# Three reorderings in a one-core Trainium2 kernel for layer norm, linear attention and an MLP

## The chip, the cores and the metric

The kernel runs as one program on one core of one Trainium2 chip. A core has four compute engines that each take their instructions in order: TensorE (PE) multiplies matrices, with its weight loads shown apart as PEld, VectorE (DVE) and ScalarE (ACT) work element by element and read PE's result banks (PSUM), and GpSimd (POOL) works element by element on the other on-chip memory (SBUF). SyncE (SP) issues the DMAs. [...] The metric is the device time of one execution in microseconds (us); a smaller number is better.

## The reference

`x` holds 2048 tokens of 640 features. Everything is float32.

```python
x = A_x
xn = _layernorm(x, axis=-1)
return x + _A_ref(xn, A_wqkv, A_w_phi, A_wo) + _B_ref(xn, B_w1, B_b1, B_w2, B_b2)

def _A_ref(x, wqkv, w_phi, wo):                    # 32 heads of 20
    qkv = (x @ wqkv).reshape(B, S, 3, H, Dh)...    # q, k, v
    pq = jnp.einsum("bhsd,hdf->bhsf", q, w_phi)
    pk = jnp.einsum("bhsd,hdf->bhsf", k, w_phi)
    phi_q = jnp.concatenate([_softmax(pq), _softmax(-pq)], axis=-1)
    phi_k = jnp.concatenate([_softmax(pk), _softmax(-pk)], axis=-1)
    kv = jnp.einsum("bhsf,bhsd->bhfd", phi_k, v)
    z  = jnp.einsum("bhsf->bhf", phi_k)
    num = jnp.einsum("bhqf,bhfd->bhqd", phi_q, kv)
    den = jnp.einsum("bhqf,bhf->bhq", phi_q, z)[..., None] + 1e-6
    return (num / den).reshape(B, S, D) @ wo

def _B_ref(x, w1, b1, w2, b2):                     # 640 -> 1728 -> 640
    y = _layernorm(x, axis=-1)
    h = _gelu(jnp.einsum("bsd,df->bsf", y, w1) + b1)
    return jnp.einsum("bsf,fd->bsd", h, w2) + b2
```

## The kernel before

Every float32 operand of a product is split into a high part (an ACT copy to the multiplication format) and a low part (source minus high part, on DVE or POOL; line 58, L1025, L959). A product is then three matmuls, high by high, high by low and low by high, and stands in the profile as lines 64, 65 and 66 (`mm3`). Tokens are worked on in four blocks of 512 (`b` = 0 to 3), or in 16 tiles of 128 (`t` = 0 to 15).

There are four stages in time.

1. The MLP for blocks 0 and 1, up to about 243 us, with the preparation of the attention weights beside it.
2. The projections to keys, values and queries, tile by tile, up to about 437 us. The list `(t, i)` in the code sets the order of PE: `i` = 0 is the main part of k, 1 the rest of k, the rest of q and part of v, 2 the rest of v, 3 the main part of q. For k, `k_tile` builds the two softmaxes: minimum and maximum on DVE (L630, L631), subtractions on POOL (L641), one exponential on ACT (L642), row sums and reciprocal on DVE (L644, L650), one product on POOL (L652), then the split into `ft` or `w1`. For q, `q_tile` does the same with its own subtractions (L641) and products (L691, L693), and transposes on DVE (L699). `kv_tile(t)` multiplies the finished features of k by v and sums them over tokens in five PSUM banks (L672) and one extra bank (L676); it runs some tiles later than the tile's projection. The sum of the last tile, `kv_tile(15)`, runs behind the first two hidden chunks of block 2.
3. The MLP for blocks 2 and 3 from about 437 to 662 us (`passes(g, b, ws)`, `g` = 0 to 6, two hidden chunks of 128 each), with the attention (`attend`, `Attention`) beside it. A hidden chunk takes 15 matmuls into one of the three banks of `ptile`, the same three that the projections use in turn, and `gelu` (L252) empties the bank.
4. The output projection from 662 us to the end (`plain`, `half_size`). Each `mm3` advances a step counter (`advance`); work of other engines is issued at given steps. Blocks 2 and 3 use sums and differences of tokens and of weights (`sums`, `weight_sums`), which save some of the products. `plain` uses two banks in turn; `gather` (L1163) adds a bank to the result on DVE, and that bank's next product waits for it.

In stages 1, 3 (from `g` = 1) and 4 the four compute engines keep the order of the code. In stage 2 and at its end only PE does; DVE, ACT and POOL are ordered there by a scheduler (SP throughout), which `tc.issue_after(x)` ties to an instruction `x`. In `finish_kv` and around it, the subtractions of the last q tile (`subs["q", 15]`) are such ties: the second part of a weight split (`late.pop()()`) and a memset of `kvs` (L809) come behind them. The first MLP pass of stage 3 is tied behind `exps["q", 15]`, the last exponential, since `gelu` needs another table on ACT.

Of the kernel before, what the change touches and what calls it, by code (L numbers as in the profile page):

```python
# [11 lines left out]
ALU = mybir.AluOpType  # L12
# [3 lines left out]
P = 128  # L16
S, D, F, H, DH = 2048, 640, 1728, 32, 20
KC = D // P
# [27 lines left out]
def tile_kernel(ctx: ExitStack, tc: tile.TileContext, x, xT, wkT, wqT, wv, wphi, wo, w1, b1, w2, b2,  # L46
                ident, mmask, emask, vsel, out):
    nc = tc.nc
# [267 lines left out]
    wc, parts, dmas = {}, {}, {}  # L316
# [266 lines left out]
    a = ExitStack()  # L583
# [8 lines left out]
    vbuf = []  # L592
# [17 lines left out]
    turn, exps, subs = [0], {}, {}  # L610
# [14 lines left out]
    def features(t, n):  # L625

        turn[0] += 1
        p3 = pks[0 if n == "k" else 1 + t % 3].rearrange("p (h f) -> p h f", f=DH)
        mx = kp.tile([P, 2, H], F32, name="mx")
        nc.vector.tensor_reduce(mx[:, 0, :], p3, axis=AX, op=ALU.max)  # L630
        nc.vector.tensor_reduce(mx[:, 1, :], p3, axis=AX, op=ALU.min)  # L631
        e = mtile(turn[0] % 3)
        e4 = e.rearrange("p s (h f) -> p s h f", f=DH)
        parts = [(slice(0, H), e4)] if n == "k" else by_head(e.rearrange("p s f -> p (s f)"), DH)
        for hs, ep in parts:
            for s, (a, b) in enumerate(((p3, mx[:, 0, :].unsqueeze(2).to_broadcast([P, H, DH])),
                                        (mx[:, 1, :].unsqueeze(2).to_broadcast([P, H, DH]), p3))):
# [3 lines left out]
                subs[n, t] = nc.gpsimd.tensor_tensor(ep[:, s], a, b, op=ALU.subtract)  # L641
        exps[n, t] = nc.scalar.activation(e, e, AF.Exp, scale=rs_all[:, t:t + 1])  # L642
        sm = kp.tile([P, 2 * H], F32, name="sm")
        nc.vector.tensor_reduce(sm, e.rearrange("p s (h f) -> p (s h) f", f=DH), axis=AX, op=ALU.add)  # L644
        return e, sm

    def k_tile(t):
        e, sm = features(t, "k")
        w = kp.tile([P, 2 * H], F32, name="w")
        nc.vector.reciprocal(w, sm)  # L650
        e3 = e.rearrange("p s (h f) -> p (s h) f", f=DH)
        nc.gpsimd.tensor_tensor(e3, e3, w.unsqueeze(2).to_broadcast([P, 2 * H, DH]), op=ALU.mult)  # L652
# [54 lines left out]
    fts, ets = {}, {}  # L707
# [3 lines left out]
    for t, i in [(t, i) for t in range(13) for i in range(4)] + [(13, 0), (13, 1), (13, 2), (14, 0), (14, 1), (13, 3), (14, 2), (15, 0), (15, 1),  # L711
                                                                  (14, 3), (15, 3), (15, 2)]:
        if (t, i) in ((4, 0), (8, 0)):
            b = t // 4 + 1
            y[b] = [yp.tile([P, KC, 512], F32R, name=f"y{p}{b % 2}") for p in range(2)]
            for p in range(2):
                nc.sync.dma_start(f(y[b][p]), y_dram[b - 2][p])
        ps = proj(t, i)
        pq = 1 + t % 3
        if i == 0:  # L720
            evac = evacuate(ps, 0, slice(1, 17))
        elif i == 1:
            evac = evacuate(ps[:, :F2], 0, slice(17, 20))
            evacuate(ps[:, F2:2 * F2], pq, slice(17, 20))
            v_parts(t, (ps[:, 2 * F2:], 0, 5, G3))
            fts[t] = k_tile(t)
        elif i == 2:
            v_parts(t, (ps[:, :15 * DH], 5, 5, G3), (ps[:, 15 * DH:17 * DH], 10, 1, 2 * DH))
        else:
            evac = evacuate(ps, pq, slice(1, 17))  # L730
            q_tile(t)

        tk = 14 if (t, i) == (15, 2) else t - 2 if t > 1 and i == 0 else None
        if tk is not None:
            kv_tile(tk, fts.pop(tk), vbuf[tk % 2])
        if t and t % 4 == 0:
            store_phi(t // 4 - 1, i)
        if i == 0 and t in (1, 2, 3, 6, 7):

            kc = (1, 2, 3, 6, 7).index(t)  # L740
            lo = rp.tile([P, D], F32, name="r1")
            hi = rp.tile([P, D], F32R, name="r2")
            nc.sync.dma_start(lo, wo[kc * P:(kc + 1) * P, :])
            with tc.issue_after(evac):
                split(hi, lo.bitcast(F32R), lo, eng=nc.gpsimd)
            for w, wd in zip((f(hi), lo), wo_dram):
                nc.sync.dma_start(wd[:, kc, :], w)
        if (t, i) == (11, 0):
            mlp = Mlp((0, 2, 3, 1), ((1, 2), (0, 3)))
            mlp.ph = ptile  # L750
            mlp.fetch(0)
        if (t, i) == (12, 3):
            with tc.issue_after(evac):
                ws = [mlp.take(0)]
            mlp.fetch(1)
        if (t, i) == (15, 3):
            w, late = mlp.take_parts(1)
            ws.append(w)
            late.pop(0)()
# [255 lines left out]
    def tokens(ap):  # L1015
        return ap.rearrange("p (q t n) -> p t q n", q=4, t=4)
# [4 lines left out]
    def hi(t, src, eng=None):  # L1021
        return lambda: nc.scalar.activation(t[0], src, AF.Copy)

    def lo(t, src, eng):
        return lambda: eng.tensor_tensor(t[1], src, f(t[0]), op=ALU.subtract)  # L1025

    def add(eng, out, a, op, b):
        return lambda: eng.tensor_tensor(out, a, b, op=op)
# [9 lines left out]
    def weight_sums(j, start):  # L1038

        w, g = weights[j], nc.gpsimd  # L1040
        if j == 0:
            for n in ("s1", "s2", "s3", "s4", "d5"):
                w[n] = own(ep.tile([P, 512], F32R, name="e", bufs=6), 1 if n == "d5" else 2)
        s = [late[1][:, i * 256:i * 256 + 256].rearrange("p (k n) -> p k n", k=2) for i in range(2)]
        a11, a12, a15, a21, a22, a25 = (late[0][:, j, c, m:m + P] for m in (0, P) for c in (k1, k2, slice(4, 5)))
        events = []
        for n, when, out, x, op, z in (("s1", 0, s[0], a21, ALU.add, a22), ("s2", 1, s[1], s[0], ALU.subtract, a11),
                                       ("s3", 6, s[0], a11, ALU.subtract, a21), ("s4", 9, s[0], a12, ALU.subtract, s[1]),
                                       ("d5", 10, s[1][:, 0:1], a15, ALU.subtract, a25)):
            when += start  # L1050
            events += [(when, add(g, out, x, op, z)), (when + 2, hi(w[n], out)), (when + 2.5, lo(w[n], out, g))]
        return at_steps(*events)

    at = {}
# [42 lines left out]
    def sums():  # L1097
# [18 lines left out]

        v = nc.vector

        def parts(at_, t, src, eng, lag):
            for k in range(2):  # L1120
                part = [by_tile(x[:, k, :]) for x in t]
                yield at_ + k, hi(part, tokens(src[:, k, :]))
                yield at_ + k + lag, lo(part, tokens(src[:, k, :]), eng)

        t1, t2, t3, t4 = tsum
        events = [(0, add(v, q[0], o3[:, k1], ALU.subtract, o2[:, k1])), (3, add(v, q[1], o3[:, k2], ALU.subtract, q[0])),
                  *parts(4, t1, q[0], v, 2), *parts(11, t2, q[1], v, 2),
                  (15, add(v, q[0], o3[:, k2], ALU.subtract, o3[:, k1])), *parts(18, t3, q[0], v, 2),
                  (17, add(v, q[1], o2[:, k2], ALU.subtract, q[1])), *parts(22, t4, q[1], v, 2)]
        return both(at_steps(*events), weight_sums(1, 8))  # L1130

    def late_split(b):
# [13 lines left out]
    def advance():  # L1146
        nonlocal step
        step += 1
        next(mlp.beside, None)
        for n, at_ in enumerate((3, 28), 1):  # L1150
            if step - at_ in range(KC + 1):
                at[n].split(step - at_, nc.vector)
        if step == 18:
            finish(mlp.beside)
            running.append(sums())
        if step == 51:
            running.append(late_split(3))
        for r in running:
            next(r, None)
# [117 lines left out]
```

## Time and profile before

| what | before |
|---|---|
| time, median of 3 runs | 734.23 us (734.23 to 734.6) |
| the profiled execution's own time | 734.7 us |
| its span, first to last instruction | 732.9 us |
| instructions | 9792 |
| DVE busy | 495.2 us (68%) |
| ACT busy | 330.3 us (45%) |
| POOL busy | 386.4 us (53%) |
| mean DMA rate | 132 GB/s |

The span is what the instructions cover; 1.8 us of the execution lie around it. Times in rows of a timeline are counted from the span's start. In such a row stand the start, the duration, the engine, the line and operation, what is written from what, shapes and a count, and in brackets how long the engine stood idle before it and what ended that. Consecutive instructions of one kind are merged into a row with a count, and how many depends on the stretch that was asked for.

### The profile page before, as it was taken

How to read it: one execution, taken by the hardware profiler on the slowest of the kernel's cores; microseconds unless marked ns; L12 is line 12 of the kernel's file. 1: busy time of each engine (PE TensorE's matmuls, PEld its weight loads, DVE VectorE, ACT ScalarE, POOL GpSimd, SP SyncE). 2: the span in 40 equal slices, each digit the busy share in tenths (PEclk: the TensorE clock that was granted, in tenths of full speed). 3: DMA queues.
4: the chain of work that ended last, by engine and by line, in shares of the span. 5: the costliest groups of instructions: out<-in, count | busy, mean ns of one | idle time of the engine just before them, and what ended most of it. 6: DMA issues, size and time to landing. Idle time of an engine off the chain costs nothing.

```text
span 732.9 us, 9792 instructions
## 1 busy us (share of the span) xinstructions
PE 718.2 (98%) x3428; PEld 602.0 (82%) x3428; DVE 495.2 (68%) x823; ACT 330.3 (45%) x567; POOL 386.4 (53%) x342
## 2 busy tenths in 40 slices
PE   8999999999999999999999996999999999999998
PEld 7788887788888888888888885888878888878787
DVE  7848445787653897897887886435565656777853
ACT  7623543434314553553544556156555556550410
POOL 2211312556103887887879789145576777543300
PEclk9999999999999999999999998999999999999999
DMA  9905466545152234534403407933433443153122
GB/s 324 268 20 158 123 194 188 175 166 205 49 216 90 90 111 131 156 134 129 97 1 68 112 18 236 251 111 112 126 108 119 119 140 108 46 226 117 72 86 87
DMA packets 67145, 96.86 MB, mean 132 GB/s; under 512 B 14656, under 2 KB 37840, under 8 KB 65472
## 3 DMA queue, kind: packets, MB, share of 16 engines
q1 hardware_dynamic: 66808, 96.23, 42.2%
q8 instruction: 27, 0.44, 0.3%
q14 instruction: 22, 0.18, 0.1%
q10 hardware_dynamic: 288, 0.01, 0.0%
HBM read 65.87 MB, written 30.35 MB: 131 GB/s over the span
## 4 chain that ended last, share of the span: by engine, by line
PE 89%; DVE 5%; ACT 3%; DMA 1%; issue 1%; POOL 1%; SPq 0%; ACTq 0%; POOLq 0%
PE bank L64 26%; PE bank L65 26%; PE bank L66 26%; PE bank L672 3%; PE bank L459 2%; PE bank L894 1%; PE bank L893 1%; DMA xb<-in_x 1%; DVE m L58 1%; DVE st L130 1%; DMA r<-in_w 1%; DVE y L959 1%; PE bank L829 1%; ACT m L252 1%; DVE y L58 0%
## 5 line engine op out<-in xcount | busy, mean ns | idle before, releaser
L58 POOL TENSOR_TENSOR w<-r,w 128x640 fp32r<-128x640 f32 x52 | 83.4, 1620 | 119.7 <-ACT w L55 90.4
L64 PE MATMUL bank<-y,w 128*128 128x512 f32 (+1 forms) x310 | 122.3, 395 | 1.2 <-DVE ob L1163 1.2
L66 PE MATMUL bank<-y,w 128*128 128x512 f32 (+1 forms) x310 | 121.1, 390 | 0.0
L65 PE MATMUL bank<-y,w 128*128 128x512 f32 (+1 forms) x310 | 120.9, 390 | 0.0
L64 PE MATMUL bank<-m,w 128*128 128x512 f32 x266 | 106.2, 399 | 2.0 <-DVE acc L297 1.3
L66 PE MATMUL bank<-m,w 128*128 128x512 f32 x266 | 104.2, 392 | 0.0
L65 PE MATMUL bank<-m,w 128*128 128x512 f32 x262 | 102.4, 391 | 0.0
L297 DVE TENSOR_TENSOR acc<-bank,acc 128x512 f32<-128x512 f32 x120 | 80.8, 682 | 17.1 <-PE bank L66 12.2
L64 PE MATMUL bank<-wkh,y 128*128 128x512 f32 (+2 forms) x240 | 87.7, 365 | 0.0
L65 PE MATMUL bank<-wkl,y 128*128 128x512 f32 (+2 forms) x240 | 87.2, 363 | 0.0
L66 PE MATMUL bank<-wkh,y 128*128 128x512 f32 (+2 forms) x240 | 86.8, 362 | 0.0
L58 DVE TENSOR_TENSOR m<-m,m 128x512 fp32r<-128x512 f32 (+1 forms) x54 | 45.3, 839 | 55.9 <-ACT m L55 55.9
L64 PEld LDWEIGHTS bank<-y,w 128*128 128x128 f32 x310 | 58.9, 190 | 13.5 <-DVE ob L1163 1.6
L66 PEld LDWEIGHTS bank<-y,w 128*128 128x128 f32 x310 | 58.6, 189 | 12.3
L65 PEld LDWEIGHTS bank<-y,w 128*128 128x128 f32 x310 | 58.8, 190 | 12.0
L641 POOL TENSOR_TENSOR m<-m,mx 128x640 f32<-128x640 f32 (+2 forms) x48 | 43.3, 917 | 42.7 <-DVE mx L630 42.7
L623 ACT ACTIVATE m<-bank 128x512 f32<-128x512 f32 (+1 forms) x64 | 26.4, 439 | 86.4 <-PE bank L66 60.6
L887 POOL TENSOR_TENSOR e<-e,m 120x512 fp32r<-120x512 f32 (+1 forms) x28 | 38.0, 1359 | 48.5 <-ACT m L886 45.7
L64 PEld LDWEIGHTS bank<-m,w 128*128 128x128 f32 x266 | 50.0, 188 | 14.4 <-DVE acc L297 3.3
L252 ACT ACTIVATE m<-bank,b1t 128x512 f32<-128x512 f32 (+1 forms) x54 | 36.2, 672 | 51.6 <-PE bank L66 49.0
L644 DVE TENSOR_REDUCE sm<-m 128x64 f32<-128x1280 f32 x32 | 47.3, 1479 | 17.9 <-ACT m L642 17.7
L66 PEld LDWEIGHTS bank<-m,w 128*128 128x128 f32 x266 | 49.9, 188 | 10.7
(211 smaller groups left out, 1483.4 us busy)
## 6 DMA issues: line engine op xcount, KB each, us to landing
r<-in_w SPq DMA_DIRECT2D x52, 320.0 KB
e<-e SPq DMA_DIRECT2D x40, 240.0 KB
e<-acc SPq DMA_DIRECT2D x52, 160.0 KB
acc<-in_xT SPq DMA_DIRECT2D x4, 1280.0 KB
xb<-in_x SPq DMA_DIRECT2D x8, 320.0 KB
t<-in_x SPq DMA_DIRECT2D x8, 320.0 KB
raw<-in_xT SPq DMA_DIRECT2D x10, 256.0 KB
yh<-t SPq DMA_DIRECT2D x10, 256.0 KB
```

Of the source, the lines that this page charges most:

```text
L58: eng.tensor_tensor(lo, src, f(hi), op=ALU.subtract)
L64: nc.tensor.matmul(ps, lh, rh, start=first, stop=False, **kw)
L65: nc.tensor.matmul(ps, lh, rl, start=False, stop=False, **kw)
L66: nc.tensor.matmul(ps, ll, rh, start=False, stop=last, **kw)
L252: nc.scalar.activation(gt, pz, AF.Gelu_apprx_tanh, bias=b1t[:, 2 * g + j:2 * g + j + 1])
L297: nc.vector.tensor_tensor(acc[b][:, m, :], pw, acc[b][:, m, :], op=ALU.add)
L459: nc.tensor.matmul(ps[:, i * kd:(i + 1) * kd], raw[:kk, (k + i) * P:(k + i + 1) * P], wpt[:kk, g, :nh, 1:], start=True, stop=True)
L623: return nc.scalar.activation(p3[:, :, c], ps.rearrange("p (h f) -> p h f", h=H), AF.Copy).ins
L641: subs[n, t] = nc.gpsimd.tensor_tensor(ep[:, s], a, b, op=ALU.subtract)
L644: nc.vector.tensor_reduce(sm, e.rearrange("p s (h f) -> p (s h) f", f=DH), axis=AX, op=ALU.add)
L672: nc.tensor.matmul(kvp[g // 2][:VM, (g % 2) * 240:(g % 2) * 240 + 240].rearrange("p (s f) -> p s f", s=4), v[:, g * VS:g * VS + VM], ft[:, ...
L887: nc.gpsimd.tensor_tensor(pl, e, f(ph), op=ALU.subtract)
```

## The change

First, the four subtractions of the last q tile are issued behind the POOL product of the last k tile (`muls[15]`). Second, `kv_tile(12)` moves from behind projection (14, 0) to behind projection (14, 1), and so takes the next bank of `ptile` for its extra sums. Third, in stage 4 the token sums and their splits are issued at other steps: from step 10 instead of 18, each sum with its two splits as a group, five steps apart; the splits of block 2 (`at[2].split`) move from steps 28 to 33 to six single steps from 31 to 41; the splits of the weight sums come 3 and 4 steps behind their sum instead of 2 and 2.5, with some sums later.

```diff
@@ features
-                subs[n, t] = nc.gpsimd.tensor_tensor(ep[:, s], a, b, op=ALU.subtract)
+                with tc.issue_after(muls[15]) if (n, t) == ("q", 15) else ExitStack():
+                    subs[n, t] = nc.gpsimd.tensor_tensor(ep[:, s], a, b, op=ALU.subtract)
@@ k_tile
-        nc.gpsimd.tensor_tensor(e3, e3, w.unsqueeze(2).to_broadcast([P, 2 * H, DH]), op=ALU.mult)
+        muls[t] = nc.gpsimd.tensor_tensor(e3, e3, w.unsqueeze(2).to_broadcast([P, 2 * H, DH]), op=ALU.mult).ins
@@ projections
         ps = proj(t, i)
+        if (t, i) == (14, 1):
+            kv_tile(12, fts.pop(12), vbuf[0])
...
-        tk = 14 if (t, i) == (15, 2) else t - 2 if t > 1 and i == 0 else None
+        tk = {(15, 2): 14, (14, 0): None}.get((t, i), t - 2 if t > 1 and i == 0 else None)
@@ weight_sums
-                                       ("s3", 6, s[0], a11, ALU.subtract, a21), ("s4", 9, s[0], a12, ALU.subtract, s[1]),
-                                       ("d5", 10, s[1][:, 0:1], a15, ALU.subtract, a25)):
+                                       ("s3", 7, s[0], a11, ALU.subtract, a21), ("s4", 12, s[0], a12, ALU.subtract, s[1]),
+                                       ("d5", 13, s[1][:, 0:1], a15, ALU.subtract, a25)):
...
-            events += [(when, add(g, out, x, op, z)), (when + 2, hi(w[n], out)), (when + 2.5, lo(w[n], out, g))]
+            events += [(when, add(g, out, x, op, z)), (when + 3, hi(w[n], out)), (when + 4, lo(w[n], out, g))]
@@ sums
-                yield at_ + k, hi(part, tokens(src[:, k, :]))
-                yield at_ + k + lag, lo(part, tokens(src[:, k, :]), eng)
+                yield at_, hi(part, tokens(src[:, k, :]))
+                yield at_ + 2 + k, lo(part, tokens(src[:, k, :]), v)
...
-        events = [(0, add(v, q[0], o3[:, k1], ALU.subtract, o2[:, k1])), (3, add(v, q[1], o3[:, k2], ALU.subtract, q[0])),
-                  *parts(4, t1, q[0], v, 2), *parts(11, t2, q[1], v, 2),
-                  (15, add(v, q[0], o3[:, k2], ALU.subtract, o3[:, k1])), *parts(18, t3, q[0], v, 2),
-                  (17, add(v, q[1], o2[:, k2], ALU.subtract, q[1])), *parts(22, t4, q[1], v, 2)]
+        events = [(1, add(v, q[0], o3[:, k1], ALU.subtract, o2[:, k1])), *parts(1, t1, q[0]),
+                  (6, add(v, q[1], o3[:, k2], ALU.subtract, q[0])), *parts(6, t2, q[1]),
+                  (11, add(v, q[0], o3[:, k2], ALU.subtract, o3[:, k1])), *parts(11, t3, q[0]),
+                  (16, add(v, q[1], o2[:, k2], ALU.subtract, q[1])), *parts(16, t4, q[1])]
@@ advance
-        for n, at_ in enumerate((3, 28), 1):
-            if step - at_ in range(KC + 1):
-                at[n].split(step - at_, nc.vector)
-        if step == 18:
+        for b, steps in ((1, (3, 4, 5, 6, 7, 8)), (2, (31, 32, 33, 36, 37, 41))):
+            if step in steps:
+                at[b].split(steps.index(step), nc.vector)
+        if step == 10:
```

POOL at the end of stage 2, before. `m_3994` are the features of k of tile 15, `m_4026` and `m_4064` those of q of tiles 14 and 15, `w_4082` is a weight chunk of the MLP.

```order
L58 TENSOR_TENSOR w_4082<-r_3729,w_4082 128x640
L641 TENSOR_TENSOR m_4064<-m_2047,mx 128x10x60
L641 TENSOR_TENSOR m_4064<-m_2047,mx 128x40
L641 TENSOR_TENSOR m_4064<-mx,m_2047 128x10x60
L641 TENSOR_TENSOR m_4064<-mx,m_2047 128x40
L58 TENSOR_TENSOR w_4082<-r_3730,w_4082 128x640
L809 MEMSET kvs 120x1408
L652 TENSOR_TENSOR m_3994<-m_3994,w 128x1280
```

The same place in the changed kernel, where the line numbers are larger by 1 to 3:

```order
L58 TENSOR_TENSOR w_4082<-r_3729,w_4082 128x640
L653 TENSOR_TENSOR m_3994<-m_3994,w 128x1280
L642 TENSOR_TENSOR m_4064<-m_2047,mx 128x10x60
L642 TENSOR_TENSOR m_4064<-mx,m_2047 128x10x60
L642 TENSOR_TENSOR m_4064<-m_2047,mx 128x40
L642 TENSOR_TENSOR m_4064<-mx,m_2047 128x40
L58 TENSOR_TENSOR w_4082<-r_3730,w_4082 128x640
L812 MEMSET kvs 120x1408
```

The product of k has moved from behind six instructions to ahead of them. On ACT at that place, before, `m_4143` are the first hidden chunks of block 2 behind `gelu`, `ft` is the high part of the features of k of tile 15, and `r_4120`, `r_4121` are loaded weights:

```order
L55 ACTIVATE w_4209<-r_4120 128x640
L642 ACTIVATE m_4064<-m_4064,rs_all 128x1280
L252 ACT_TABLE_LOAD
L252 ACTIVATE m_4143<-bank_4145,b1t 128x512
L252 ACTIVATE m_4143<-bank_4165,b1t 128x512
L55 ACTIVATE m_4164<-m_4143 128x512
L55 ACTIVATE ft<-m_3994 128x1280
```

And in the changed kernel:

```order
L643 ACTIVATE m_4026<-m_4026,rs_all 128x1280
L55 ACTIVATE ft<-m_3994 128x1280
L643 ACTIVATE m_4064<-m_4064,rs_all 128x1280
L252 ACT_TABLE_LOAD
L252 ACTIVATE m_4143<-bank_4145,b1t 128x512
L252 ACTIVATE m_4143<-bank_4165,b1t 128x512
L803 ACTIVATE t_4199<-bank_2022 127x480
```

The copy of `ft` now stands ahead of the last exponential and of the table load, and the copy of the loaded weights `r_4120` stands further back, where the two rows of `w_4209` follow the hidden chunks. On SP the two 1280 KB loads of `acc` (L300) now stand ahead of the load of `r_4120` (L214) instead of behind it; the stores of the q features (L705) follow as before, save that the load of `r_4215` (L215), ahead of all of them before, now stands behind the third.

DVE in stage 4, before; L1163 are the additions to the result, L1028 the sums of tokens, L1025 the splits of the sums, L959 the splits of block 2:

```order
L1163 TENSOR_TENSOR ob_6059<-bank_6139,ob_6059 128x512
L959 TENSOR_TENSOR y_6152<-acc_5095,y_6151 128x512
L1025 TENSOR_TENSOR m_6104<-w_6097,m_6100 128x512
L959 TENSOR_TENSOR y_6152<-acc_5095,y_6151 128x512
L1025 TENSOR_TENSOR m_6104<-w_6097,m_6100 128x512
L959 TENSOR_TENSOR y_6152<-acc_5095,y_6151 128x512
L1028 TENSOR_TENSOR w_6097<-acc_5433 128x1024
L1028 TENSOR_TENSOR w_6097<-acc_5095,w_6097 128x1024
L1163 TENSOR_TENSOR ob_6059<-bank_6172,ob_6059 128x512
```

In the changed kernel, from the second to the sixth addition (here L1166; L1031 are the sums, L1028 the splits):

```order
L1166 TENSOR_TENSOR ob_5948<-bank_6044,ob_5948 128x512
L1031 TENSOR_TENSOR w_6067<-acc_5433,acc_5095 128x1024
L1028 TENSOR_TENSOR m_6073<-w_6067,m_6069 128x512 x2
L1166 TENSOR_TENSOR ob_5948<-bank_6079,ob_5948 128x512
L1031 TENSOR_TENSOR w_6067<-acc_5433,w_6067 128x1024
L1028 TENSOR_TENSOR m_6074<-w_6067,m_6070 128x512 x2
L1166 TENSOR_TENSOR ob_5948<-bank_6102,ob_5948 128x512
L1031 TENSOR_TENSOR w_6067<-acc_5433 128x1024
L1028 TENSOR_TENSOR w_6068<-w_6067,m_6071 128x512 x2
L1166 TENSOR_TENSOR ob_5948<-bank_6127,ob_5948 128x512
L1031 TENSOR_TENSOR w_6067<-acc_5095,w_6067 128x1024
L1028 TENSOR_TENSOR w_6068<-w_6067,m_6072 128x512 x2
```

Where up to seven instructions stood between two additions, there is now one sum and its two splits between each two.

More of the change, by code (lines that the diff above doesn't have):

```diff
@@ L608, in proj @@
         return ps
-    turn, exps, subs = [0], {}, {}
+    turn, exps, subs, muls = [0], {}, {}, {}
     pks = [m[:, i, :] for m in (mtile(3), mtile(4)) for i in range(2)]
@@ L1117, in sums, with parts @@
         v = nc.vector
-        def parts(at_, t, src, eng, lag):
+        def parts(at_, t, src):
             for k in range(2):
                 part = [by_tile(x[:, k, :]) for x in t]
-                yield at_ + k, hi(part, tokens(src[:, k, :]))
-                yield at_ + k + lag, lo(part, tokens(src[:, k, :]), eng)
+                yield at_, hi(part, tokens(src[:, k, :]))
+                yield at_ + 2 + k, lo(part, tokens(src[:, k, :]), v)
         t1, t2, t3, t4 = tsum
-        events = [(0, add(v, q[0], o3[:, k1], ALU.subtract, o2[:, k1])), (3, add(v, q[1], o3[:, k2], ALU.subtract, q[0])),
-                  *parts(4, t1, q[0], v, 2), *parts(11, t2, q[1], v, 2),
-                  (15, add(v, q[0], o3[:, k2], ALU.subtract, o3[:, k1])), *parts(18, t3, q[0], v, 2),
-                  (17, add(v, q[1], o2[:, k2], ALU.subtract, q[1])), *parts(22, t4, q[1], v, 2)]
+        events = [(1, add(v, q[0], o3[:, k1], ALU.subtract, o2[:, k1])), *parts(1, t1, q[0]),
+                  (6, add(v, q[1], o3[:, k2], ALU.subtract, q[0])), *parts(6, t2, q[1]),
+                  (11, add(v, q[0], o3[:, k2], ALU.subtract, o3[:, k1])), *parts(11, t3, q[0]),
+                  (16, add(v, q[1], o2[:, k2], ALU.subtract, q[1])), *parts(16, t4, q[1])]
         return both(at_steps(*events), weight_sums(1, 8))
```

## The prediction

> **What bounds the kernel.** I read the cores' spans and the page's first part, then what PE waited for.
>
> ```profile
> core 0: 732.9 us, clock 0.995
> ```
>
> ```profile
> PE 718.2 (98%) x3428; PEld 602.0 (82%) x3428; DVE 495.2 (68%) x823; ACT 330.3 (45%) x567; POOL 386.4 (53%) x342
> ```
>
> ```profile
> PE bank L672 <- DVE ft L58: 5.5, 1, 5.5
> ...
> PE bank L64 <- DVE acc L297: 1.3, 1, 1.3
> PE bank L64 <- DVE ob L1163: 1.2, 1, 1.2
> ...
> PE bank L672 <- DVE w L58: 0.5, 1, 0.5
> ```
>
> PE is the bound: it is busy for 718.2 of 732.9 us, and no matmul is removed. What can be won is its waits (us in total, count, longest) and what they bring after them. The change touches all four rows. Next, matmuls around three of these waits, and the granted clock.
>
> ```profile
> 407.24 0.39 PE L66 MATMUL bank<-wkh,y 128*128 128x512 f32 x1
> 408.15 1.38 PE L672 MATMUL bank<-w,v 128*127 128x240 f32 x10 [0.52 <-DVE w L58]
> ...
> 409.44 0.42 PE L64 MATMUL bank<-wkh,y 128*128 128x492 f32 x1
> ...
> 436.86 0.43 PE L64 MATMUL bank<-y,w 128*128 128x512 f32 x1
> ...
> 443.47 0.39 PE L66 MATMUL bank<-y,w 128*128 128x512 f32 x1
> 449.39 2.49 PE L672 MATMUL bank<-ft,v 128*127 128x240 f32 x10 [5.53 <-DVE ft L58]
> ...
> 455.73 0.42 PE L64 MATMUL bank<-y,w 128*128 128x512 f32 x1
> ...
> 689.52 0.39 PE L66 MATMUL bank<-y,r 128*128 128x512 f32 x1
> 691.12 0.50 PE L64 MATMUL bank<-y,w 128*128 128x512 f32 x1 [1.22 <-DVE ob L1163]
> ```
>
> ```profile
> 443.70:449.40 5.70, 0.17 (x2) 0.01 (x1) 4.50 (x5) 3.88 (x5) 5.70 (x7) 0.96 0.97 370
> 449.40:455.20 5.80, 5.80 (x19) 5.12 (x20) 5.32 (x10) 3.26 (x6) 5.13 (x6) 0.50 0.25 70
> ...
> 689.70:691.10 1.40, 0.21 (x1) 0.00 (x0) 1.40 (x3) 1.40 (x5) 0.20 (x1) 1.00 0.00 0
> ```
>
> The 30 matmuls from 436.86 start 6.61/29 = 0.228 us apart. So PE was free at 443.70 and stood until 449.39. Then it ran at half speed: in a row of the second fence the granted clock is the third number from the end, 0.50 from 449.40 to 455.20, but 1.00 over the short wait for `ob`. The key sum of tile 12 takes 1.29 us (408.15 to 409.44). That of tile 15 and nine matmuls more are 1.29 + 9 x 0.228 = 3.34 us of work, and took 6.34 (449.39 to 455.73). The largest wait thus costs 5.69 us, and 3.00 more through the clock.
>
> **What the largest wait hangs on.** POOL, ACT and DVE there, and earlier rows of the same kinds:
>
> ```profile
> 415.63 1.28 POOL L641 TENSOR_TENSOR m<-mx,m 128x640 f32<-128x640 f32 x1
> ...
> 426.09 2.72 POOL L693 TENSOR_TENSOR m<-m,w 128x600 f32<-128x600 f32 x2
> ...
> 434.89 1.58 POOL L58 TENSOR_TENSOR w<-r,w 128x640 fp32r<-128x640 f32 x1 [0.30 <-ACT w L55]
> 436.42 1.43 POOL L641 TENSOR_TENSOR m<-m,mx 128x600 f32<-128x600 f32 x2
> 437.81 1.42 POOL L641 TENSOR_TENSOR m<-mx,m 128x600 f32<-128x600 f32 x2
> ...
> 441.92 2.37 POOL L652 TENSOR_TENSOR m<-m,w 128x1280 f32<-128x1280 f32 x1
> ```
>
> ```profile
> 441.23 0.74 ACT L55 ACTIVATE w<-r 128x640 fp32r<-128x640 f32 x1 [3.95 <-DMA r<-in_w]
> 441.87 1.35 ACT L642 ACTIVATE m<-m,rs_all 128x1280 f32<-128x1280 f32 x1
> 443.24 1.28 ACT L252 ACT_TABLE_LOAD   x1
> 444.54 1.27 ACT L252 ACTIVATE m<-bank,b1t 128x512 f32<-128x512 f32 x2
> ...
> 446.37 1.25 ACT L55 ACTIVATE ft<-m 128x1280 fp32r<-128x1280 f32 x1
> ```
>
> ```profile
> 415.78 2.48 DVE L58 TENSOR_TENSOR ft<-m,ft 128x1280 fp32r<-128x1280 f32 x1 [0.46 <-ACT ft L55]
> ...
> 426.02 1.49 DVE L58 TENSOR_TENSOR w<-m,w 128x1280 fp32r<-128x1280 f32 x1 [0.37 <-ACT w L55]
> ...
> 435.70 0.54 DVE L650 RECIPROCAL w<-sm 128x64 f32<-128x64 f32 x1
> ```
>
> The reciprocal is done at 436.24, but its product L652 starts at 441.92, behind the subtractions of the last q, a weight split and the memset. ACT's copy to `ft` and DVE's split follow it, the copy behind exponential, table load and `gelu` too.
>
> **Key sum of tile 12.** PE stood from 407.47 to 408.15 for it. Projection (14, 1) now takes that place, with a bank emptied long before, and the sum's features are ready under its cover. Gain 0.68; without the cover, nothing.
>
> **Product ahead of subtractions.** The product can start when the weight split ends (436.47). What feeds both runs 0.2 to 0.7 earlier, as PE does; I take 436.1, so 438.4 at its end. The copy to `ft` (1.25) ends at 439.7. DVE's split then comes among POOL's subtractions, and there the two engines shut each other out: 2.48 instead of 1.49 beside POOL's row at 415.63, and POOL's 2.72, beside DVE's split at 426.02, where subtractions of the same two shapes take 1.43. So I put them one behind the other: 438.4 + 1.43 + 1.42 + 1.5 = 442.8 for the last subtraction. The split itself, behind the second subtraction, ends by 442.4. PE comes to the last key sum at 443.70 - 0.68 = 443.02 and does not wait for it.
>
> Late next is a bank. Three serve in turn, so behind the sum (443.02 + 1.29 = 444.3) the first hidden chunk of block 3 needs the bank that the first `gelu` empties, and that stands behind the last exponential, which needs the last subtraction. Exponential, table load and one `gelu` took 444.54 + 0.64 - 441.87 = 3.3 us; hence 442.8 + 3.3 = 446.1 and a wait of 1.8. Its ends are 0 (product and subtractions begin 0.4 earlier and do not collide: 444.2) and 2.7 (the product at 436.5 and one weight split of 0.5 in between). Nine matmuls on, PE stands at 446.1 + 9 x 0.228 = 448.2, where it stood at 455.73. With the key sum of tile 12 that is **7.5 us**.
>
> [...]
>
> Queued behind the `gelu`s on ACT are copies of key banks and hidden chunks, then weight copies that wait for loads. Their first user, the second layer of block 2, is due at 446.1 + 6.8 = 452.9; five copies (2.8 us) and two DVE splits fit behind 446.8. On SP the loads of `acc` go ahead of that of `r`, and are first used behind that layer: nothing. The stores of q features start only about 1 us earlier, but their reloads serve products some 25 us later: nothing, by up to 1.
>
> **Stage 3's end.** ACT there:
>
> ```profile
> 645.84 0.85 ACT L1022 ACTIVATE e<-wos 128x256 fp32r<-128x256 f32 x2 [1.67 <-POOL wos L1028]
> 646.60 2.18 ACT L957 ACTIVATE y<-ob 128x512 fp32r<-128x512 f32 x4
> 648.80 0.69 ACT L252 ACTIVATE m<-bank,b1t 128x512 f32<-128x512 f32 x1
> ```
>
> The `gelu` at 648.80 leads, through DVE, to the wait of 1.3 for `acc`. One of the four copies ahead of it (0.55) now fills ACT's idle 1.67. Between 0 and 0.6 of it arrives: **0.3**.
>
> **Stage 4.** DVE, ACT and POOL:
>
> ```profile
> 673.56 1.22 DVE L1028 TENSOR_TENSOR w<-acc,acc 128x1024 f32<-128x1024 f32 x1
> ...
> 678.09 1.29 DVE L1025 TENSOR_TENSOR m<-w,m 128x512 fp32r<-128x512 f32 x2
> ...
> 690.39 0.68 DVE L1163 TENSOR_TENSOR ob<-bank,ob 128x512 f32<-128x512 f32 x1
> ```
>
> ```profile
> 674.87 1.15 ACT L1022 ACTIVATE m<-w 128x512 fp32r<-128x512 f32 x2 [18.77 <-DVE w L1028]
> ```
>
> ```profile
> 682.17 0.74 POOL L1025 TENSOR_TENSOR w<-wos,w 128x256 fp32r<-128x256 f32 x1 [0.41 <-ACT w L1022]
> ```
>
> Before, PE is free at 689.75 and waits 1.37 for the addition at 690.39, late behind seven instructions. Now each addition follows one sum, the first of its two copies on ACT, and two splits: 1.22 + 0.58 + 1.29 + 0.68 = 3.8 us a group, where a product takes 15 x 0.228 = 3.42. The first group starts behind product (0, 1), 6 products before 689.75, and its addition: 669.2 + 0.9 = 670.1. Four groups end at 685.3; the bank is due one product before 689.75, at 686.3. Of the spare 1.0, POOL's weight splits and sums (0.74 each) take some by the same exclusion: none to four, up to 3.0. I take 1.2, hence a wait of 0.2 in place of 1.37: **1.2** (ends -0.6 and 1.4).
>
> **Sum.** 7.5 + 0.3 + 1.2 = 9.0 of the profiled execution's 734.7 (732.9 of span and 1.8 around it): 725.7. It stands 0.5 above the median of the runs, 734.23, so I predict **725.2**.
>
> **Rivals.**
> - *No wait at the bank*: the row 441.92 would speak for it, where nothing delays the exponential but POOL; 1.8 less, 723.4. Against it: two collisions above. Chance 0.18.
> - *DVE falls behind in stage 4*: 3.8 against 3.42 a product speaks for it; against it, only four groups. Up to 2.1 of wait instead of 0.2: 726.4 to 727.1. Chance 0.14.
> - *The clock halves all the same*, because the key sum and the bank make PE stand about 3.5 us in a row of short waits: 1.7 more of wait and 3.0 for the clock, 729.9; with the forecast's wait alone 728.2. Against it, 1.00 over the wait at 689.70. Chance 0.08. [...]
> - *Slower*: ACT waits in order for the load of `r`, now behind 2560 KB of `acc`. Row 441.23 shows 3.95 of such a wait. Behind it stand the `gelu`s of block 3, and on DVE the additions that free the banks of block 2's second layer, due about 459. [...] The DMA share of 0.97 before 449.40 and 0.25 behind it speaks against. Chance 0.03.
> - *The change does not do what it says*: the product stays late, since POOL waits at the weight split for ACT (0.30 at 434.89). It would have to stand 6 us; then 733 to 735. Chance 0.03.
>
> The forecast has 0.50, and 0.04 is left for waits in between. The range 723.2 to 727.4 holds the forecast with its ends, the first two rivals, and 0.82 in all. Faster by over 0.2% (1.5 us, about what a measurement of this kernel tells from no change) 0.94, same 0.03, slower 0.03.
>
> **What would show it.** The row of PE's waits for `ft` is gone; instead one for ACT `m` at the bank of block 3 of about 1.8, with the clock at 1.00 throughout; L653 on POOL right behind the weight split, near 436; no wait for `w` at the key sum of tile 12; that for `ob` below 0.5. A clock of 0.50 near 450, or a DVE wait above 1.4 in stage 4, would make the prediction wrong.

## The result, and the profile after

The changed kernel takes **726.62 us** (726.18 to 727.05) beside 734.23 for the kernel before: ratio 0.9896, 95% interval 0.9879 to 0.9913. The forecast was 725.2, in a range of 723.2 to 727.4. The profiled execution took 726.96 with a span of 725.2. Of the four executions two have a span of 725.2 and 725.3 at a mean granted clock of 0.997 and 0.998, and two have 724.5 and 724.4 at 1.000. That pair of values is what the forecast lacked. One execution in a later repeat of this kernel took 1844.35 with its matmuls stretched (0.83 us each at line 64 in the largest group, beside 0.39), and is left out everywhere.

First the core's span, then what PE waited for (us in total, times, longest), both of the changed kernel:

```profile
core 0: 725.2 us, clock 0.997
```

```profile
PE bank L64 <- ACT m L252: 1.8, 1, 1.8
PE bank L366 <- POOL m L364: 1.3, 1, 1.3
PE bank L64 <- DVE acc L297: 0.9, 1, 0.9
PE bank L64 <- DVE acc L295: 0.6, 1, 0.6
PE bank L173 <- DVE xb L164: 0.4, 1, 0.4
```

The rows for `ft`, for `w` at the key sum of tile 12 and for `ob` are gone. In their place stands one for `m` of ACT, the bank of block 3. The timeline of POOL, DVE and ACT around it (start, us, engine, line, operation):

```profile
436.27 2.37 POOL L653 TENSOR_TENSOR m<-m,w 128x1280 f32<-128x1280 f32 x1 [0.28 <-DVE w L651]
438.60 1.21 POOL L642 TENSOR_TENSOR m<-m,mx 128x600 f32<-128x600 f32 x1
439.77 1.21 POOL L642 TENSOR_TENSOR m<-mx,m 128x600 f32<-128x600 f32 x1
440.94 1.50 POOL L642 TENSOR_TENSOR m<-m,mx 128x40 f32<-128x40 f32 x1
442.40 0.25 POOL L642 TENSOR_TENSOR m<-mx,m 128x40 f32<-128x40 f32 x1
```

```profile
439.99 2.34 DVE L58 TENSOR_TENSOR ft<-m,ft 128x1280 fp32r<-128x1280 f32 x1 [0.81 <-ACT ft L55]
```

```profile
442.68 1.37 ACT L643 ACTIVATE m<-m,rs_all 128x1280 f32<-128x1280 f32 x1 [2.73 <-POOL m L642]
444.07 1.28 ACT L252 ACT_TABLE_LOAD   x1
445.36 1.27 ACT L252 ACTIVATE m<-bank,b1t 128x512 f32<-128x512 f32 x2
```

DVE's split (source minus high part) is released at 439.99 but ends only at 442.33, so it takes 2.34, where a split of as many elements took 1.49 at 426.02 in the kernel before: POOL is in its second subtraction until 440.98. Then POOL's third, of 40 columns, takes 1.50, beside 0.25 for the fourth, of the same shape, behind the split; the split holds it off. PE in the same place, and the windows of 1 us over it (the number behind the five engines is the granted clock):

```profile
442.96 1.28 PE L673 MATMUL bank<-ft,v 128*127 128x240 f32 x10
444.08 0.24 PE L677 MATMUL bank<-ft,v 128*107 128x160 f32 x1
446.10 0.51 PE L64 MATMUL bank<-y,w 128*128 128x512 f32 x1 [1.79 <-ACT m L252]
...
447.38 0.63 PE L66 MATMUL bank<-y,w 128*128 128x512 f32 x1
...
449.09 0.63 PE L64 MATMUL bank<-y,w 128*128 128x512 f32 x1
```

```profile
446.00:447.00 1.00, 0.90 (x4) 0.76 (x5) 1.00 (x5) 1.00 (x4) 1.00 (x2) 1.00 1.05 397
447.00:448.00 1.00, 1.00 (x5) 0.82 (x4) 1.00 (x4) 1.00 (x4) 1.00 (x4) 0.68 0.56 210
448.00:449.00 1.00, 1.00 (x4) 0.80 (x3) 1.00 (x3) 1.00 (x4) 1.00 (x2) 0.50 0.00 0
449.00:450.00 1.00, 1.00 (x4) 0.72 (x3) 1.00 (x3) 1.00 (x3) 0.62 (x2) 0.50 0.00 0
450.00:451.00 1.00, 1.00 (x4) 0.79 (x3) 1.00 (x3) 0.30 (x1) 1.00 (x1) 0.62 0.00 0
```

Up to 447 the clock is full; then it is halved for (0.32 + 0.50 + 0.50 + 0.38) x 2 = **3.40 us**. Nine matmuls behind the start of block 3, PE stands at 449.09 instead of the 448.2 forecast, and some more of the half speed is still to come. How far PE is ahead further on, at the end of the key normalisation and at the wait for `acc` that ends stage 3, first the kernel before, then the changed one:

```profile
471.74 0.48 PE L64 MATMUL bank<-m,w 128*128 128x512 f32 x1
...
655.62 0.50 PE L64 MATMUL bank<-m,w 128*128 128x512 f32 x1 [1.28 <-DVE acc L297]
```

```profile
465.86 0.48 PE L64 MATMUL bank<-m,w 128*128 128x512 f32 x1
...
649.38 0.50 PE L64 MATMUL bank<-m,w 128*128 128x512 f32 x1 [0.93 <-DVE acc L297]
```

Stage 4, DVE:

```profile
663.32 0.69 DVE L1166 TENSOR_TENSOR ob<-bank,ob 128x512 f32<-128x512 f32 x1
663.92 1.22 DVE L1031 TENSOR_TENSOR w<-acc,acc 128x1024 f32<-128x1024 f32 x1
665.90 1.29 DVE L1028 TENSOR_TENSOR m<-w,m 128x512 fp32r<-128x512 f32 x2 [0.76 <-ACT m L1025]
667.11 0.69 DVE L1166 TENSOR_TENSOR ob<-bank,ob 128x512 f32<-128x512 f32 x1
...
677.22 1.76 DVE L1028 TENSOR_TENSOR w<-w,m 128x512 fp32r<-128x512 f32 x2 [0.70 <-ACT m L1025]
678.89 0.68 DVE L1166 TENSOR_TENSOR ob<-bank,ob 128x512 f32<-128x512 f32 x1
```

From addition to addition a group takes 667.11 - 663.32 = 3.79, and one in four 4.19, with its splits at 1.76 instead of 1.29. PE no longer waits for `ob`.

### The profile page after: what moved, and what is told of

It reads as the page before. It is cut to its first block, busy times and chain, and to the rows that moved or that the text cites. A ratio compares the mean times of both kernels' runs of the same rounds, so it can differ in the third digit from the quotient of the medians.

```text
span 725.2 us, 9793 instructions
## 1 busy us (share of the span) xinstructions
PE 716.7 (99%) x3428; PEld 601.8 (83%) x3428; DVE 494.2 (68%) x823; ACT 330.8 (46%) x567; POOL 388.1 (54%) x342
## 4 chain that ended last, share of the span: by engine, by line
PE 79%; POOL 7%; DVE 7%; ACT 3%; issue 2%; SPq 1%; DMA 1%; DVEq 0%; POOLq 0%; ACTq 0%
PE bank L64 24%; PE bank L66 23%; PE bank L65 23%; POOL m L642 3%; PE bank L459 2%; PE bank L897 1%; POOL m L653 1%; PE bank L896 1%; PE bank L673 1%; SPq L706 1%; DVE st L130 1%; POOL w L692 1%; DVE acc L700 1%; DMA e<-acc 1%; POOL m L694 1%
## 5 line engine op out<-in xcount | busy, mean ns | idle before, releaser
L297 DVE TENSOR_TENSOR acc<-bank,acc 128x512 f32<-128x512 f32 x120 | 81.0, 683 | 17.7 <-PE bank L66 12.7
L58 DVE TENSOR_TENSOR m<-m,m 128x512 fp32r<-128x512 f32 (+1 forms) x54 | 43.6, 810 | 53.0 <-ACT m L55 53.0
L64 PEld LDWEIGHTS bank<-m,w 128*128 128x128 f32 x266 | 50.0, 188 | 14.0 <-DVE acc L297 2.9
L66 PEld LDWEIGHTS bank<-m,w 128*128 128x128 f32 x266 | 49.9, 188 | 10.7
L65 PEld LDWEIGHTS bank<-m,w 128*128 128x128 f32 x262 | 49.3, 188 | 9.9
```

The source lines that it names most:

```text
L58: eng.tensor_tensor(lo, src, f(hi), op=ALU.subtract)
L64: nc.tensor.matmul(ps, lh, rh, start=first, stop=False, **kw)
L65: nc.tensor.matmul(ps, lh, rl, start=False, stop=False, **kw)
L66: nc.tensor.matmul(ps, ll, rh, start=False, stop=last, **kw)
L297: nc.vector.tensor_tensor(acc[b][:, m, :], pw, acc[b][:, m, :], op=ALU.add)
```

## The experiments

Eleven runs, in three lots. A lot ran on one chip and shared its runs of the kernel before (medians 734.36, 733.65 and 734.48).

### The three parts, each alone

`e1_product_only` is the kernel before with this edit:

```diff
...
-                subs[n, t] = nc.gpsimd.tensor_tensor(ep[:, s], a, b, op=ALU.subtract)
+                with tc.issue_after(muls[15]) if (n, t) == ("q", 15) else ExitStack():
+                    subs[n, t] = nc.gpsimd.tensor_tensor(ep[:, s], a, b, op=ALU.subtract)
...
```

> Only the product of the last k ahead of the subtractions of the last q; the key sum of tile 12 and stage 4 stand as before. Theory (the bank of block 3 sets the end, so PE starts block 3 at the same moment with or without the earlier key sum): PE comes to the last key sum near 443.7 and, behind it, waits about 1.2 instead of 1.8; block 3 starts near 446.2; the gain is 6.2 to 7.8 and the time 726.5 to 728.0, with the wait of 1.2 for ob still there. Rival (the parts add up): 7.6 less 1.4 of stage 4 and less 0.7 of the key sum is 5.5, so 728.7. A halved clock behind the wait is possible under both, and less likely than behind 1.8.

Measured 728.03 (727.44 to 730.65). PE comes to the last key sum at 443.61, waits 1.19 at the bank and starts block 3 at 446.15, beside 446.10 in the changed kernel: the theory, though the median is 0.03 above its range. All four mean clocks are 0.999 or 1.000. The longest execution is the profiled one. In it, ACT waited until 479.03 for the first reloaded q features, and PE stood for them:

```profile
PE bank L64 <- DVE acc L297: 2.8, 2, 1.5
PE bank L366 <- POOL m L364: 1.3, 1, 1.3
PE bank L64 <- DVE ob L1164: 1.2, 1, 1.2
PE bank L64 <- ACT m L252: 1.2, 1, 1.2
...
PE bank L895 <- POOL e L888: 0.8, 1, 0.8
```

One of the two waits of L297, 1.5 at 494.80, and that of L895, 0.8 at 481.06, are new. They come up beside the first attention of stage 3, which uses these features.

`e2_sum12_only` is the kernel before with this edit:

```diff
+        if (t, i) == (14, 1):
+            kv_tile(12, fts.pop(12), vbuf[0])
...
-        tk = 14 if (t, i) == (15, 2) else t - 2 if t > 1 and i == 0 else None
+        tk = {(15, 2): 14, (14, 0): None}.get((t, i), t - 2 if t > 1 and i == 0 else None)
```

> Only the key sum of tile 12 one bank later. Theory (what the last key sum waits for hangs on POOL, not on PE): the wait of 0.5 for w is gone, that for ft grows by about the same, and the time is 733.7 to 734.2. Rival (the prediction's term, a gain of 0.68 that reaches the end): 733.5.

Measured 732.12 (731.60 to 732.55), ratio 0.9971 (0.9960 to 0.9981): 2.2 faster, more than either said. The wait for `ft` shrank from 5.5 to 4.6 although PE came 0.83 earlier, since the last split ended 1.7 earlier. The reason is ACT's order in that kernel:

```profile
444.32 1.25 ACT L55 ACTIVATE ft<-m 128x1280 fp32r<-128x1280 f32 x1
447.45 1.54 ACT L55 ACTIVATE w<-r 128x640 fp32r<-128x640 f32 x2 [1.87 <-DMA r<-in_w]
```

Before, a weight copy that waits for its load stood ahead of the last exponential, and the copy to `ft` came at 446.37. With the key sum elsewhere the scheduler puts the weight copy behind. So this part alone also moves ACT, and its gain is not that of the key sum.

`e3_stage4_only` is the kernel before with the events of stage 4 of the change (`weight_sums`, `sums`, `advance`), for example:

```diff
-        if step == 18:
+        if step == 10:
```

> Only the events of stage 4 (token sums, weight sums, splits of block 2 at fixed places). Theory: the wait for ob (1.37 with what it takes to start again) is gone and nothing takes its place, so 732.8; DVE's groups show splits of 1.29 with one of about 1.8. Rival (DVE falls behind in groups of 3.8): a wait of 0.2 to 2.1 is left, 733.0 to 735.

Measured 731.99 (731.54 to 732.95), ratio 0.9971 (0.9961 to 0.9981). The wait for `ob` is gone, and nothing came in its place. That for `acc` at the end of stage 3 fell from 1.28 to 0.93, which the expectation left out. The two profiled spans differ by 732.9 - 731.2 = 1.7, that is 1.37 + 0.35.

The three gains alone are 6.3, 2.2 and 2.4, together 10.9; the change as a whole brings 7.6. So the parts overlap: the first and the third add up (8.7, beside 8.6 for `e9` below, which is the change without the second), and what the second brings alone is not added to them.

### The bank, the clock and the reload

`e4_gelu_first` is the changed kernel with the rest of the last q (from its exponential on) traced behind the first `gelu` of block 2, at the cost of two more table loads (1.28 us each in the row at 444.07):

```diff
...
     def last_kv():
-        for _ in range(12):
+        for _ in range(5):
+            yield
+        with tc.issue_after(mlp.last_gelu):
+            q_tile(15, e15)
+        mlp.gelu_after = exps["q", 15].ins
+        for _ in range(7):
             yield
...
```

> The changed kernel, and in it the first gelu of block 2 ahead of the last exponential (two table loads more on ACT). Theory (the 1.8 at the bank is all that stands there, and the half clock behind it comes from it): no wait for m at block 3, granted clock 1.00 in every execution, block 3 starts near 444.3; 1.8 and up to 1.6 less, so 722.8 to 724.6. Rival 1: the second gelu, now behind one more table load, is late for the next bank and the wait moves there: 725 to 726.6. Rival 2: the half clock comes from the short key sum and not from the wait: the wait goes, the clock stays at 0.50 in some executions, 724.8 or so.

Measured 726.02 (725.68 to 726.25). Its first half is as the theory has it: no wait at the bank, the clock at 0.999 or 1.000 in all four, and PE 465.86 - 462.17 = 3.7 ahead of the changed kernel at the last matmuls of the key normalisation. Of that, only 1.3 is left at the end of stage 3, for the loss that `e1` showed is here too:

```profile
PE bank L64 <- DVE acc L299: 2.3, 2, 1.3
...
PE bank L911 <- POOL e L904: 0.6, 1, 0.6
```

```profile
476.14 0.63 ACT L903 ACTIVATE m<-e 80x512 fp32r<-80x512 f32 x1 [4.83 <-DMA e<-e]
```

ACT is idle for 4.83 until the features of q land at 476.14. The theory has the clock and block 3 right and the time wrong; the time lies in the first rival's range, but its wait is not there. None of the three named this place. A new theory: the reload of block 0's features, queued behind stores, weight loads and two loads of `woc` (the output weights for stage 4, 1280 KB), sets a floor under stage 3, and what PE gains beyond it is lost. `e6` and `e7` try it.

`e5_changed_again` has no edit.

> The changed kernel once more, for the spread of its clock. Theory: the wait of 1.8 halves the clock in some executions (span 725.2, mean clock 0.997 or 0.998) and not in others (724.4, 1.000), both again; since half speed over 3.1 us costs PE 1.6 but the spans differ by 0.8, an execution at full clock shows about 0.8 of waits between 478 and 495 that the profiled one does not have. Rival: the 0.8 goes at the end of stage 3 (wait for acc at 649 grows from 0.9 to 1.7), nothing new near 480.

Its profile is of the execution left out above and can't answer. The other three have spans of 725.4 at 0.997, 723.5 at 0.999 and 725.2 at 0.999. The last doesn't fit two groups: half speed over 3.4 us alone gives a mean of 0.998, so a mean of 0.999 leaves no room for it, and what made this execution longer is open.

`e6_woc_later` is the changed kernel, with those two loads issued behind the reloads:

```diff
...
+            if (g, b) == (2, 2):
+                with tc.issue_after(at[0].loaded.ins):
+                    for j in range(2):
+                        nc.sync.dma_start(late[0][:, j], wo.rearrange("(c p) n -> p c n", p=P)[:, :, 256 * j:256 * j + 256])
...
-                for j in range(2):
-                    nc.sync.dma_start(late[0][:, j], wo.rearrange("(c p) n -> p c n", p=P)[:, :, 256 * j:256 * j + 256])
```

> The changed kernel with the two loads of woc (1280 KB, first read in stage 4) issued behind the reloads of the q features of block 0 instead of ahead of them. Theory (the reload is what waits in the DMA queues, and takes back what PE gains): executions at full clock reach a span of 723.6 (time 725.4), those at half clock stay at 725.2 (727.0). Rival (the loss is elsewhere): full-clock spans stay at 724.4.

Spans of 725.2 and 725.2 at 0.998, and of 723.5 and 723.6 at 1.000: the theory, to 0.1. The two groups differ by 1.65, which is what half the speed over 3.4 us costs (3.4 / 2 = 1.7). This alone does not settle it, though: on the same chip one execution of the changed kernel without the edit (`e5`) had a span of 723.5 too, and the execution of `e6` that was profiled is one at half clock. Median 726.15.

`e7_gelu_and_woc` is both edits together.

> The first gelu ahead of the last exponential, and the loads of woc behind the reloads. Theory: without the load of 1280 KB ahead of them the features land 3 to 4 us earlier, the waits for e (0.6) and acc (1.3) near 478 and 491 go, and the 726.0 of the first gelu alone becomes 723.8 to 724.4. Rival (these waits come from ACT and POOL, which work through the features in order, and not from the DMA): 725.8 to 726.2.

Measured **723.43** (723.37 to 723.48), ratio 0.9860 (0.9845 to 0.9875), 10.2 below the kernel before in the same lot and the fastest here. What PE waits for:

```profile
PE bank L368 <- POOL m L366: 1.3, 1, 1.3
PE bank L64 <- DVE acc L299: 0.9, 1, 0.9
PE bank L64 <- DVE acc L297: 0.6, 1, 0.6
PE bank L173 <- DVE xb L164: 0.4, 1, 0.4
```

The waits near 478 and 491 are gone, and ACT takes up the third group of features at 473.04, after 0.53 of idle time for the DMA, where `e4` had it at 477.60. So they came from the DMA and not from the order on ACT and POOL. The gains over the kernel before, each in its own lot, are 8.3 for `e4` and 10.2 here, and the two waits were 0.6 + 1.3 = 1.9. The median is 0.4 below the theory's range.

`e8_split_behind` is the changed kernel, with DVE's split of the last k held until the last subtraction of q has written its result:

```diff
...
+            with tc.issue_after(nc.vector.tensor_copy(one, ep[:, 1, 1, 19:20]).ins):
+                nc.vector.tensor_tensor(lo, x, hi_, op=ALU.subtract)
...
```

> The changed kernel, and DVE's split of the last k held back until the last subtraction of q is done (a copy of one element that reads the last subtraction's result stands ahead of it). Theory (the two shut each other out, so the split costs the subtractions 1.25): the four subtractions take 1.21, 1.21, 0.25 and 0.25, the last ends near 441.5 instead of 442.65; the split takes 1.4 instead of 2.34 and ends near 443.1; the last key sum waits 0.1 to 0.4 for ft, the bank 0.3 to 0.6 instead of 1.8, clock 1.00; 725.2 to 726.3. Rival (the third subtraction is slow by itself): it takes 1.5 again, the last ends near 442.6, the key sum waits 1.3 and the bank 1.5: 727.5.

Measured 725.46 (725.11 to 725.51), clock 1.000 in all four. POOL and DVE:

```profile
438.66 1.21 POOL L643 TENSOR_TENSOR m<-m,mx 128x600 f32<-128x600 f32 x1
439.83 1.21 POOL L643 TENSOR_TENSOR m<-mx,m 128x600 f32<-128x600 f32 x1
440.99 0.26 POOL L643 TENSOR_TENSOR m<-m,mx 128x40 f32<-128x40 f32 x1
441.20 0.26 POOL L643 TENSOR_TENSOR m<-mx,m 128x40 f32<-128x40 f32 x1
441.41 1.58 POOL L58 TENSOR_TENSOR w<-r,w 128x640 fp32r<-128x640 f32 x1
```

```profile
441.56 2.77 DVE L648 TENSOR_TENSOR ft<-m,ft 128x1280 fp32r<-128x1280 f32 x1
```

Alone, the third subtraction takes 0.26, and the last ends at 441.46: the theory. But the split is no shorter. It now meets POOL's weight split and takes 2.77, so the key sum waits 1.2 for `ft` where 0.1 to 0.4 was expected, and the bank not at all. PE starts block 3 at 445.69, only 0.41 earlier than in the changed kernel; of the 1.9 between the two profiled spans (725.2 and 723.3) 1.5 is left, which fits the 1.7 of the half speed. So the time is in the theory's range, but not by the way that the theory gave.

### How long a wait halves the clock

`e9_without_sum12` is the changed kernel, with the key sum of tile 12 back at its old place (the diff of `e2` undone).

> The changed kernel with the key sum of tile 12 back at its old place. Theory (the bank sets when block 3 starts, and the clock is judged over stretches of 3.4 us, as long as the stretch at half speed in the profile; a wait of 1.2 leaves each of them busy enough): PE starts block 3 at 446.1 to 446.2 all the same, behind a wait of 1.2 instead of 1.8, full clock in every execution, 725.3 to 726.3, thus no slower than the changed kernel and steadier. Rival (the 0.68 of the key sum is a gain that reaches the end): 727.3.

`e10_copy_behind_exp` is the changed kernel with one more copy on ACT:

```diff
+        if (n, t) == ("q", 15):
+            exps[n, t] = nc.scalar.activation(e, e, AF.Copy)
```

> The changed kernel, and on ACT one copy of 1.3 us more, of the last exponential's result onto itself, ahead of the gelu. Theory (the longer PE stands, the more surely one stretch of 3.4 us has too little work): the bank of block 3 is waited for 3.0 to 3.4 instead of 1.8, and every execution shows a stretch at half clock (mean clock 0.998 or below), none 1.000; 728.3 to 729.5. Rival (the clock falls by chance at any such wait): executions at full clock still appear, with 726.7 to 727.5.

`e11_changed_third` has no edit.

> The changed kernel unedited, beside the two others, for its spread on the same chip: spans of 725.2 with mean clock 0.997 or 0.998, and of 723.5 to 724.5 with 1.000. Theory of the reload: an execution at full clock above 724.2 shows waits for e or acc between 478 and 495.

Measured: `e9` 725.93 (725.72 to 726.27), mean clocks 0.999 and 1.000; `e11` 727.14 (727.02 to 727.33), 0.998 in all four. PE in `e9`:

```profile
443.73 1.28 PE L673 MATMUL bank<-ft,v 128*127 128x240 f32 x10
444.85 0.24 PE L677 MATMUL bank<-ft,v 128*107 128x160 f32 x1
446.28 0.50 PE L64 MATMUL bank<-y,w 128*128 128x512 f32 x1 [1.19 <-ACT m L252]
```

Without the earlier key sum PE comes 0.77 later and starts block 3 only 0.18 later (446.28, beside 446.10 in the changed kernel). It then runs at full speed, and the kernel is **1.2 faster** than the changed one in the same lot, whose four executions were all halved. The rival's 727.3 is out.

`e10` took 729.66 (728.99 to 730.21), above what was expected in three of five executions, since the wait became 3.9 and not 3.0 to 3.4 (the scheduler put two copies of key banks ahead of the table load as well). Its mean clock is 0.998 in three executions and 0.995 in two, never 1.000. `e11` had no execution at full clock, so its sentence on the reload was not tried.

All runs by the wait of PE between the first hidden chunks of block 2 and those of block 3, at the last key sum or behind it, as the profiled execution of each kernel shows it:

| wait of PE (us) | kernels | executions | mean granted clock |
|---|---|---|---|
| 0 | e4, e7 | 8 | 0.999 or 1.000 |
| 1.2 | e1, e8 (at the key sum), e9 | 12 | 0.999 or 1.000 |
| 1.8 | changed kernel (with e5, e11), e6 | 15 | 0.997 or 0.998 in 9, 0.999 or 1.000 in 6 |
| 3.9 | e10 | 5 | 0.998 in 3, 0.995 in 2 |
| 4.6 | e2 (at the key sum) | 8 | 0.998 in 3, 0.994 or 0.995 in 5 |
| 5.5 | before (beside these runs), e3 (at the key sum) | 43 | 0.993 to 0.995 |

Half speed over 3.41 us takes 0.0024 from a mean over 725 us. Half speed at the very end, when the last matmul is done, costs nothing and takes 0.0009 in the changed kernel (723.83 to 725.2). So 0.997 and 0.998 stand for one such piece, 0.994 and 0.995 for two, and 0.993, in one execution of the kernel before (736.2 us), for three. A mean of 0.999 leaves no room for one; what lowers it from 1.000 in `e9` and `e7` is not shown.

## Why the prediction was right, point by point

**Product ahead of subtractions: right to 0.2 us.** The product started at 436.27 (436.1 forecast), the last subtraction ended at 442.65 (442.8), PE came to the last key sum at 442.96 (443.02) and did not wait, the bank was free after a wait of 1.79 (1.8), and block 3 began at 446.10 (446.1). The order was the forecast one too: the split, behind the second subtraction, ended at 442.33 (442.4), and one engine's time added to the other's, which is what the step rests on. Two small errors cancel: the split held POOL up for 1.25 and not 1.5, and the product ended at 438.64 and not at 438.4. `e8` shows the cause: without the split beside it, the row of 1.50 takes 0.26.

**Key sum of tile 12: the place was right, the gain was not one.** The wait for `w` went and PE was 0.7 earlier at the last key sum. But the bank frees at its own time, and of the 0.68 only 0.18 arrived; the rest lengthened the wait there (1.19 in `e9`, 1.79 with it). The forecast's joint 7.5 took this in, since it runs through the bank; "Gain 0.68" beside it did not stand. With the clock, the move costs 1.2 where every execution with it is halved, as in the lot of `e9` and `e11`; the two executions of the result at full clock (726.18 and 726.27) are level with `e9`.

**The clock: the term that failed.** The forecast kept it "at 1.00 throughout", because it was 1.00 over the wait of 1.37 for `ob`, and gave a halved clock a chance of 0.08. In the profiled execution PE is 471.74 - 465.86 = 5.88 ahead of the kernel before at the end of the key normalisation, not 7.5. The missing 1.62 is the half speed over 3.40 us, to 0.1 (3.40 / 2 = 1.70). The prediction had named a clock of 0.50 near 450 as a sign that it is wrong, and by their mean clocks two of the four executions were so; this step failed. The rival had the mechanism but priced it with the 3.00 of a wait three times as long, hence 728.2. That the time is in the range all the same is in part luck: the piece cost 1.6 and not 3.0, two executions had none, and the upper end of the range had been drawn for DVE falling behind in stage 4.

**Reload: "nothing, by up to 1"; right where it was profiled, for another reason.** Not the stores' earlier start but PE's matters: PE comes to these products earlier, by 3.7 from the changed kernel to `e4`, the features do not: ACT takes the first at 475.32 and at 476.14, after 0.32 and 4.83 of idle time for the DMA. At half clock PE is late enough not to meet it: the profiles of the changed kernel, `e6` and `e11` show no wait there. In `e4`, further ahead, it took 1.9. What it takes from the changed kernel at full clock is not shown: its spans there are 724.5, 724.4, 723.5 and 725.2, beside 723.5 and 723.6 in `e6`, and none of the four was profiled. At full clock `e8` met no such wait, `e9` one of 0.2, `e1` three.

**Stage 3's end and stage 4: right.** The wait for `acc` fell by 0.35 (0.3 forecast). That for `ob` was 1.37 and is 0 (1.2 forecast); groups take 3.79 beside the 3.8 worked out, and one collision came where up to four were allowed.

**The sum.** 5.88 + 0.36 (655.62 to 649.38, less the 5.88) + 1.37 = 7.6 of the span's 7.7, against 9.0. What is short is the clock's 1.62, less 0.2 that stages 3 and 4 brought beyond their terms. Where clock and load are both out of the way, in the better executions of `e6`, the span of 723.5 is 8.3 below the middle one of the kernel before in that lot (731.8).

## What to carry to other kernels

A gain ahead of a wait counts only as far as the thing waited for moves too (here 0.18 of 0.68 arrived); follow it through the next bank and the next reload before adding it up. Where PE is the bound, compare the wait that is left with the shortest one that has halved the clock in any run, here 1.8: in the lot that compared them, an earlier arrival at the same bank made the kernel slower (727.14 beside 725.93). When PE gets faster, look at each load that its later stages need, and at what stands ahead of it in the same queue without being needed yet (here the loads of `woc`: gains of 8.3 in `e4` and 10.2 in `e7`).

## What the hardware did that was not expected

- Half speed came in pieces of one length. Summed as above over windows of 0.5 us, it is 3.41 us in the changed kernel and in `e6`, and 6.83, twice that, in the kernel before and in `e2`. By the same windows, a piece begins 1.3 behind the end of the wait in the changed kernel (447.35), 0.3 behind it in `e6` (446.26), and in the kernel before 0.46 ahead of it (448.93), while PE still stands:

```profile
448.50:449.00 0.50, 0.00 (x0) 0.00 (x0) 0.50 (x1) 0.00 (x0) 0.50 (x1) 0.93 0.87 330
```

  What is regular is the distance from that start to the half clock behind the last matmul: 723.83 - 447.35 = 276.48 in the changed kernel and 732.24 - 448.93 = 283.31 before. In pieces of 3.41 that is 81.08 and 83.08, next to 81 and 83, which make the piece 3.413 in both. So in these two traces the starts keep one beat, and the wait falls at different points of it.
- A wait of 1.8 halved the clock in 9 of 15 executions, one of 1.2 in none of 12. If the span is cut along that beat, an estimate from these traces puts the limit near half a piece, at 1.7 of 3.41. PE stood for 1.79 of one piece in the changed kernel and for 1.81 in `e6` and `e11`, and the next was at half speed; it stood for 1.66 before (443.86 to 445.52), and the next was at full speed. A wait of 1.47 in `e1` (493.33 to 494.80) brought no half speed either: the mean clock of that execution is 1.000. The limit need not be sharp: by the same beat PE stood for about 1.8 behind the last matmul of `e11` (722.0), and the mean clock of 0.998 leaves no room for half speed there. In the kernel before, PE stood for only 0.46 of the first piece at half speed, and the second was at half speed too. That a wait of 1.8 which falls across two pieces leaves the clock full would account for the other 6 of 15; none of those was profiled. That the clock is judged over stretches of 3.4 us, as the theories of `e9` and `e10` have it, is an estimate from the length of a piece; no run shows what the chip counts, or whether narrow matmuls count in full.
- The time at which the reloaded features reached ACT differs between executions of nearly the same program, 479.03 in `e1` and 476.46 in `e9`. The execution of 725.2 at 0.999 in `e5` may be of that kind; it was not profiled.
